# Softmax attention on one core: transposes in 32-bit words, a fused shift on GpSimd, and load groups of 8 heads

## The chip, the core and the metric

The kernel runs on one core of a Trainium2 chip. A core has five engines that run side by side, each with its own instruction queue: TensorE (PE; its weight loads are listed apart as PEld), VectorE (DVE), ScalarE (ACT), GpSimd (POOL) and SyncE (SP). In this kernel SP issues all transfers between the device's memory and the on-chip memory (SBUF). TensorE writes its results to PSUM, which VectorE and ScalarE can read; GpSimd works on SBUF alone. The metric is the time of one execution in microseconds on the device. Three runs of the kernel before gave 1264.91, 1265.55 and 1264.91 us, median 1264.91.

## The reference

```
B, H, Sq, Sk, D = 16, 32, 192, 1024, 128        # q, k, v are bf16
scale  = D ** -0.5
scores = einsum("bhqd,bhkd->bhqk", q, k) * scale
p      = softmax(scores, axis=-1)
out    = einsum("bhqk,bhkd->bhqd", p, v)
```

There are 16 x 32 = 512 heads. Each has 192 queries, 1024 keys and a depth of 128.

## The kernel before, in words

**Units.** Two heads a and b make a pair; there are 256 pairs, and each pair is three units of 128 query rows: the first 128 queries of a, the first 128 of b, and the last 64 of a together with the last 64 of b. That makes 768 units. In the third unit the two heads sit in the two column halves of TensorE (`tile_position`).

**What happens to a unit.** (1) `qk`: TensorE computes 128 x 1024 scores into one of two PSUM buffers `s_ps` (lines 215, 222, 228). (2) `rowmax`: VectorE multiplies them by minus the scale, writes them to SBUF as fp32 (`ss`), and keeps each row's minimum in `nb`, all in one instruction (line 300). (3) The shift: a unit of type W (the first two of a pair, `R_W`) has `nb` subtracted on GpSimd, which writes bf16 to `x_sb` (line 188); a unit of type E (the third, `R_EA`) gets its exponential on ScalarE, which also sums the rows into `rs` (line 356). (4) `tr`: TensorE transposes `x_sb` in eight 128 x 128 pieces of bf16 into one of two PSUM buffers `pt_ps`, by a matmul with the identity as the moving operand (line 244). Piece t holds every eighth key, from t on. (5) `evac`: ScalarE brings the transposed unit back to SBUF as `pt_sb`: type W with the exponential (line 367), type E as a copy (line 369). (6) `pv`: TensorE multiplies by V (lines 267, 273, 275), and for type W also by a column of ones, which gives the row sums (line 270). (7) `onorm`: once a pair is complete, VectorE takes two reciprocals of the row sums (line 327), waits for them, and multiplies the pair's 128 x 384 results by them into the output buffer `ob` (line 330).

**Order.** There is no planner; the order is written out by hand. TensorE goes through steps: in a step it issues the scores of the next unit, the transposes of the unit four steps back and the second matmul of the unit seven steps back. The lags `L_X, L_TR, L_EV, L_PV` are 2, 4, 5 and 7; the rings of buffers `ss`, `x_sb` and `pt_sb` have as many slots as the lags need. Semaphores tie the engines: scores of unit u wait for `rowmax` of u - 2, GpSimd waits for `rowmax` and for the transposes four units back, the second matmul of a pair's first unit waits for `onorm` two pairs back.

**Loads and stores.** SP works in groups of 16 heads (`G=16`), 32 groups, with two slots (`NS=2`). For each group it issues K as a transposing transfer of 4 MB (line 141), q as a transposing transfer (line 144), and V as a plain one of 4 MB (line 149), then the stores of an earlier group (lines 158, 163, 164). K and q of a group wait until the scores of the group two before have been computed, V until its second matmul has; the stores wait for `onorm`.

Of the kernel before, what the change touches and what calls it, by code (L numbers as in the profile page):

```python
# [6 lines left out]
F32 = mybir.dt.float32  # L7
ACT_FN = mybir.ActivationFunctionType
ALU = mybir.AluOpType

R_EA = 0
R_ED = 1
R_W = 2


def _attention_kernel(nc, q, k, v, out, G=16, NS=2, LAGS=(2, 4, 5, 7), ROUTES=(R_W, R_W, R_EA)):
# [4 lines left out]
    assert NH % G == 0 and G % 2 == 0  # L21
# [3 lines left out]
    NU = NGR * UPG  # L25
    KT_TILES = SK // 128
    scale = float(D) ** -0.5

    L_X, L_TR, L_EV, L_PV = LAGS
    assert 1 <= L_X < L_TR < L_EV < L_PV  # L30
# [4 lines left out]
    NRS = 4  # L35

# [5 lines left out]
    def route(u):  # L42
        return ROUTES[u % len(ROUTES)]

    x_cnt = []
    ev_cnt = []
    n_xa = n_xp = n_ea = n_ed = 0
    for u in range(NU):
        r = route(u)
        if r == R_W:  # L50
            n_xp += 1
            x_cnt.append(n_xp)
        else:
            n_xa += 1
            x_cnt.append(n_xa)
        if r == R_ED:
            n_ed += 1
            ev_cnt.append(n_ed)
        else:
            n_ea += 1  # L60
            ev_cnt.append(n_ea)

    with ExitStack() as es:
# [11 lines left out]
        vs = sb("vs", [128, NS, G, KT_TILES, 128], BF16)  # L75
        ob = sb("ob", [128, NSO, PPG, 4, 128], BF16)
# [3 lines left out]
        pt_sb = sb("pt_sb", [128, NPT, KT_TILES, 128], BF16)  # L80
# [3 lines left out]
        ident = sb("ident", [128, 128], BF16)  # L84
        s_ps = [ps("s_ps%d" % i, [128, SK], F32) for i in range(2)]
        pt_ps = [ps("pt_ps%d" % i, [128, KT_TILES, 128], BF16) for i in range(2)]
        o_ps = [ps("o_ps%d" % i, [128, 4, 128], F32) for i in range(2)]
        s_setup = sem("s_setup")
        sxk = [sem("sxk%d" % i) for i in range(NS)]
# [5 lines left out]
        s_xa = sem("s_xa")  # L95
        s_xp = sem("s_xp")
        s_tr = sem("s_tr")
        s_eva = sem("s_eva")
        s_evd = sem("s_evd")
# [6 lines left out]
        def unit_info(u):  # L106
            pr = u // 3
            k3 = u % 3
            g = pr // PPG
            pg = pr % PPG  # L110
            return pr, k3, g, pg

        O_SLOT = (0, 2, 1)

        def load_cnt(g):
            return 16 * (g // NS + 1)

        def store_cnt(g):
            return 48 * (g // NSO + 1)

        def wait_x(eng, u):
            if route(u) == R_W:
                eng.wait_ge(s_xp, x_cnt[u])
            else:
                eng.wait_ge(s_xa, x_cnt[u])

        def wait_evac(eng, u):
            if route(u) == R_ED:
                eng.wait_ge(s_evd, ev_cnt[u])
            else:  # L130
                eng.wait_ge(s_eva, ev_cnt[u])

        @block.sync
        def _(e):
            def loads(g):
                s = g % NS
                last_u = (g - NS + 1) * UPG - 1
                h0 = g * G
                if g >= NS:
                    e.wait_ge(s_qk, last_u + 1)  # L140
# [6 lines left out]
                if g >= NS:  # L147
                    e.wait_ge(s_pv, last_u + 1)
                e.dma_start(
                    vs[:, s], vf[h0:h0 + G].rearrange("g (p t) d -> p g t d", t=KT_TILES)  # L150
                ).then_inc(svl[s], 16)

            def stores(g):
                so = g % NSO
                e.wait_ge(s_on, (g + 1) * PPG)
                h0 = g * G
                og = of[h0:h0 + G]
# [10 lines left out]
            for g in range(NGR):  # L168
                if g + NS < NGR:
                    loads(g + NS)  # L170
                stores(g)
            for so in range(min(NSO, NGR)):
                n_uses = len(range(so, NGR, NSO))
                e.wait_ge(sst[so], 48 * n_uses)

        @block.gpsimd
        def _(gp):
            gp.memset(ones[:], 1.0).then_inc(s_setup, 1)
            gp.wait_ge(s_setup, 1)
            gp.affine_select(  # L180
                ident[:], ones[:], [[1, 128]], ALU.is_equal, 0.0, base=0, channel_multiplier=-1
            ).then_inc(s_setup, 1)

            def shift(u):
                gp.wait_ge(s_max, u + 1)
                if u >= NX:
                    gp.wait_ge(s_tr, u - NX + 1)
                gp.tensor_tensor(  # L188
                    x_sb[:, u % NX, :], ss[:, u % NSS, :],
                    nb[:, u % NSS: u % NSS + 1].to_broadcast([128, SK]), ALU.subtract,  # L190
                ).then_inc(s_xp, 1)

            for u in range(NU):
                if route(u) == R_W:
                    shift(u)

        @block.tensor
        def _(pe):
            def qk(u):
                pr, k3, g, pg = unit_info(u)  # L200
                s = g % NS
                if u % UPG == 0:
                    pe.wait_ge(sxk[s], load_cnt(g))
                    pe.wait_ge(sxq[s], load_cnt(g))
# [6 lines left out]
                for c in range(2):  # L211
                    cs = slice(512 * c, 512 * c + 512)
                    if k3 < 2:
                        x = a if k3 == 0 else b
                        ins = pe.matmul(  # L215
                            S[:, cs],
                            qt[:, s, x * SQ: x * SQ + 128],
                            kt[:, s, x * SK + 512 * c: x * SK + 512 * c + 512],
                            start=True, stop=True,
                        )  # L220
                    else:
                        pe.matmul(  # L222
                            S[0:64, cs],
                            qt[:, s, a * SQ + 128: a * SQ + 192],
                            kt[:, s, a * SK + 512 * c: a * SK + 512 * c + 512],
                            start=True, stop=True, tile_position=(0, 0),
                        )
                        ins = pe.matmul(  # L228
                            S[64:128, cs],
# [6 lines left out]
            def tr(u):  # L236
                wait_x(pe, u)
                if u >= 2:
                    wait_evac(pe, u - 2)
# [176 lines left out]
```

## Time and profile before

| what | value |
|---|---|
| median of the three runs | 1264.91 us |
| the profiled execution: span from first to last instruction | 1263.1 us |
| instructions recorded | 48,658, of them 40,960 on TensorE |
| mean granted TensorE clock | 0.999 |
| moved by transfers | 321.89 MB, mean 255 GB/s |

The profile is one execution taken apart. Busy time of an engine is the time in which at least one of its instructions is running. The chain of waits is followed back from the last instruction, at each step to what released it. A line such as "POOL x_sb L188 <- PE pt_ps L244: 266.8, 254, 1.1" says that line 188 on GpSimd stood idle 266.8 us in all, 254 times and at most 1.1 us, until line 244's matmul was done. A line of the timeline gives start, duration, engine, source line, operation and result<-inputs. In a table by stretches of time, each engine has its busy time and the number of its instructions, and then come the granted clock, the share of the transfer engines and the rate in GB/s.

### The profile page before, as it was taken

The numbers are of one execution on the slowest core, as the hardware profiler recorded it, in microseconds if no ns is written. First come the engines' busy times: TensorE is split into PE (matmuls) and PEld (weight loads), VectorE is DVE, ScalarE is ACT, GpSimd is POOL, SyncE is SP. The second block draws the span as 40 slices with busy tenths as digits, with TensorE's granted clock in tenths as the row PEclk, the third lists the DMA queues.
The fourth block names the chain that finished last, engine by engine and source line by source line (L and its number), as shares of the span: only waits on it lengthen the run. The fifth ranks groups of instructions, "written<-read, shape, count | busy, mean of one in ns | idle before, by whom it ended". The sixth has DMA issues, their size and how long they took to land.

```text
span 1263.1 us, 48658 instructions
## 1 busy us (share of the span) xinstructions
PE 1234.2 (98%) x20480; PEld 1009.4 (80%) x20480; DVE 1102.0 (87%) x2304; ACT 1048.6 (83%) x1281; POOL 960.4 (76%) x518
## 2 busy tenths in 40 slices
PE   3999999999999999999999999999999999999997
PEld 1888888888888888888888888888888888888886
DVE  2889888898988989898898988889898898989885
ACT  1888888888888888888888888888888888888886
POOL 2778777777877778787777877777787777878774
PEclk9999999999999999999999999999999999999999
DMA  9999999999999999999999999999999999999941
GB/s 288 268 261 240 278 280 266 288 270 245 254 269 261 279 233 255 281 275 262 261 230 272 271 276 268 252 251 272 272 267 281 253 263 252 271 261 281 244 118 27
DMA packets 790743, 321.89 MB, mean 255 GB/s; under 512 B 724992, under 2 KB 724992, under 8 KB 790528
## 3 DMA queue, kind: packets, MB, share of 16 engines
q1 hardware_dynamic: 790528, 318.78, 108.8%
q8 instruction: 164, 2.69, 0.8%
q14 instruction: 51, 0.42, 0.1%
HBM read 134.22 MB, written 25.17 MB: 126 GB/s over the span
## 4 chain that ended last, share of the span: by engine, by line
PE 97%; SPq 1%; DMA 1%; ACT 0%; issue 0%; DVE 0%; ACTq 0%
PE pt_ps L244 33%; PE o_ps L267 24%; PE s_ps L215 18%; PE o_ps L273 11%; PE s_ps L222 9%; SPq L141 1%; DMA vs<-in_v_dram 1%; PE o_ps L270 1%; PE o_ps L275 1%; SPq L144 0%; PE s_ps L228 0%; ACT x_sb L356 0%; ACT pt_sb L367 0%; DVE ob L330 0%; DVE rinv L327 0%
## 5 line engine op out<-in xcount | busy, mean ns | idle before, releaser
L188 POOL TENSOR_TENSOR x_sb<-ss,nb 128x1024 bf16<-128x1024 f32 x512 | 959.7, 1895 | 288.9 <-PE pt_ps L244 266.8
L300 DVE TENSOR_SCALAR_CACHE_REDUCE ss<-s_ps 128x1024 f32<-128x1024 f32 x768 | 938.5, 1222 | 140.5 <-PE s_ps L215 110.8
L244 PEld LDWEIGHTS pt_ps<-ident,x_sb 128*128 128x128 bf16 x6144 | 487.1, 148 | 203.3 <-issue 105.4
L367 ACT ACTIVATE pt_sb<-pt_ps 128x1024 bf16<-128x1024 bf16 x512 | 521.0, 1018 | 41.9 <-PE pt_ps L244 41.8
L244 PE MATMUL pt_ps<-ident,x_sb 128*128 128x128 bf16 x6144 | 520.7, 228 | 0.2 <-ACT pt_sb L367 0.2
L267 PE MATMUL o_ps<-vs,pt_sb 128*128 128x128 bf16 x4096 | 403.0, 217 | 0.3 <-DMA vs<-in_v_dram 0.3
L369 ACT ACTIVATE pt_sb<-pt_ps 128x1024 bf16<-128x1024 bf16 x256 | 262.1, 1024 | 140.1 <-PE pt_ps L244 140.0
L270 PE MATMUL o_ps<-ones,pt_sb 128*128 128x1 bf16 x4096 | 376.0, 165 | 0.0
L267 PEld LDWEIGHTS o_ps<-vs,pt_sb 128*128 128x128 bf16 x4096 | 352.3, 97 | 0.5 <-DMA vs<-in_v_dram 0.4
L270 PEld LDWEIGHTS o_ps<-ones,pt_sb 128*128 128x128 bf16 x4096 | 340.7, 96 | 0.0
L215 PE MATMUL s_ps<-kt,qt 128*128 128x512 bf16 x1024 | 305.3, 379 | 21.3 <-DMA qt<-in_q_dram 21.0
L356 ACT ACTIVATE x_sb<-ss,nb 128x1024 bf16<-128x1024 f32 x256 | 292.3, 1142 | 23.6 <-DVE ss L300 23.6
L273 PE MATMUL o_ps<-vs,pt_sb 128*64 128x128 bf16 x2048 | 162.3, 222 | 0.0
L275 PE MATMUL o_ps<-vs,pt_sb 128*64 128x128 bf16 x2048 | 162.3, 222 | 0.0
L222 PE MATMUL s_ps<-kt,qt 128*64 128x512 bf16 x512 | 153.2, 381 | 0.6 <-DVE ss L300 0.5
L228 PE MATMUL s_ps<-kt,qt 128*64 128x512 bf16 x512 | 153.2, 381 | 0.0
L330 DVE TENSOR_TENSOR ob<-o_ps,rinv 128x384 bf16<-128x384 f32 x256 | 142.7, 557 | 8.7
L273 PEld LDWEIGHTS o_ps<-vs,pt_sb 128*64 128x64 bf16 x2048 | 121.0, 109 | 17.1
L275 PEld LDWEIGHTS o_ps<-vs,pt_sb 128*64 128x64 bf16 x2048 | 121.0, 109 | 0.0
L215 PEld LDWEIGHTS s_ps<-kt,qt 128*128 128x128 bf16 x1024 | 63.3, 96 | 23.6 <-issue 21.5
L300 DVE DVE_READ_ACCUMULATOR ss<-s_ps 128x1 f32 x768 | 64.0, 83 | 0.0
L356 ACT ACTIVATION_READ_ACCUMULATOR x_sb<-ss,nb 128x1 f32 x256 | 48.9, 191 | 0.0
(11 smaller groups left out, 165.7 us busy)
## 6 DMA issues: line engine op xcount, KB each, us to landing
vs<-in_v_dram SPq DMA_DIRECT2D x32, 4096.0 KB, 15.2
out_dram<-ob SPq DMA_DIRECT2D x32, 512.0 KB, 15.9
out_dram<-ob SPq DMA_DIRECT2D x64, 128.0 KB, 4.9
kt<-in_k_dram SPq DMA_TRANSPOSE x32, 21.4
qt<-in_q_dram SPq DMA_TRANSPOSE x32, 6.6
```

Of the source, the lines that this page charges most:

```text
L188: gp.tensor_tensor(x_sb[:, u % NX, :], ss[:, u % NSS, :], nb[:, u % NSS: u % NSS + 1].to_broadcast([128, SK]), ALU.subtract,).then_inc(s_x ...
L215: ins = pe.matmul(S[:, cs], qt[:, s, x * SQ: x * SQ + 128], kt[:, s, x * SK + 512 * c: x * SK + 512 * c + 512], start=True, stop=True,)
L222: pe.matmul(S[0:64, cs], qt[:, s, a * SQ + 128: a * SQ + 192], kt[:, s, a * SK + 512 * c: a * SK + 512 * c + 512], start=True, stop=True, ...
L244: ins = pe.transpose(PT[:, t, :], X[:, t: SK: KT_TILES], ident[:])
L267: ins = pe.matmul(O[:, sl, :], PTS[:, t, :], vs[:, s, x, t, :], start=first, stop=last, skip_group_check=True)
L270: ins = pe.matmul(O[:, 3, sl: sl + 1], PTS[:, t, :], ones[:, 0:1], start=False, stop=last, skip_group_check=True)
L273: pe.matmul(O[0:64, sl, :], PTS[:, t, 0:64], vs[:, s, a, t, :], start=first, stop=last, skip_group_check=True, tile_position=(0, 0))
L275: ins = pe.matmul(O[64:128, sl, :], PTS[:, t, 64:128], vs[:, s, b, t, :], start=first, stop=last, skip_group_check=True, tile_position=(0, ...
L300: dve.tensor_scalar(ss[:, u % NSS, :], s_ps[u % 2][:], -scale, None, ALU.mult, ALU.min, accum_out=nb[:, u % NSS: u % NSS + 1],).then_inc(s ...
L356: act.activation(x_sb[:, u % NX, :], ss[:, u % NSS, :], ACT_FN.Exp, bias=nb[:, u % NSS: u % NSS + 1], scale=-1.0, accum_out=rs[:, pr % NRS ...
L367: act.activation(pt_sb[:, u % NPT], pt_ps[u % 2][:], ACT_FN.Exp, scale=-1.0).then_inc(s_eva, 1)
L369: act.activation(pt_sb[:, u % NPT], pt_ps[u % 2][:], ACT_FN.Copy).then_inc(s_eva, 1)
```

## The change

**32-bit transposes.** `x_sb` and `pt_ps` are looked at as 32-bit words of two bf16 values each, and a unit is transposed in four 128 x 128 pieces of fp32 with an fp32 identity. Piece t holds every fourth word, that is keys in pairs; a transposed row holds (even key, odd key) side by side for each query. The exponential of a type W unit separates them: it reads every second bf16 value and writes the even and the odd keys as blocks. A type E unit is copied as 512 int32 words, and its second matmul reads the weights with a stride of two instead.

**Self-test.** Before the first unit, GpSimd writes index patterns, TensorE transposes two blocks of them as fp32, ScalarE copies the result as words, and VectorE compares it with the pattern expected. The outcome, 1 or 0, is written into the matrix of ones that yields the row sums. TensorE's first scores wait for it.

**Shift.** GpSimd's subtraction becomes one instruction with one tensor input: times minus one, plus the row's `nb` taken as a per-partition operand. ScalarE's exponential of type W drops its scale of minus one.

**VectorE.** The reciprocals of a pair stay where they were in the order; the multiplication by them comes one step later, behind the next `rowmax`.

**Load groups.** K, q and V come in 64 groups of 8 heads with four slots (`G=8, NS=4`) instead of 32 groups of 16 with two. The stores stay at 16 heads (`GO=16`).

```diff
-def _attention_kernel(nc, q, k, v, out, G=16, NS=2, LAGS=(2, 4, 5, 7), ROUTES=(R_W, R_W, R_EA)):
+def _attention_kernel(nc, q, k, v, out, G=8, NS=4, GO=16, L_X=2, L_TR=4, L_EV=5, L_PV=7):
...
-        ident = sb("ident", [128, 128], BF16)
+        ident = sb("ident", [128, 128], F32)
...
-                stores(g)
+                if (g + 1) % (GO // G) == 0:
+                    stores((g + 1) // (GO // G) - 1)
...
+            gp.iota(za[:, 0], [[257, 128]], base=1, channel_multiplier=32767).then_inc(s_setup, 1)
+            gp.iota(zb[:, 0], [[32767, 128]], base=1, channel_multiplier=257).then_inc(s_setup, 1)
+            gp.iota(za[:, 1], [[257, 128]], base=1060000001, channel_multiplier=32767).then_inc(s_setup, 1)
+            gp.iota(zb[:, 1], [[32767, 128]], base=1060000001, channel_multiplier=257).then_inc(s_setup, 1)
...
-                gp.tensor_tensor(
+                gp.tensor_scalar(
                     x_sb[:, u % NX, :], ss[:, u % NSS, :],
-                    nb[:, u % NSS: u % NSS + 1].to_broadcast([128, SK]), ALU.subtract,
-                ).then_inc(s_xp, 1)
+                    -1.0, nb[:, u % NSS: u % NSS + 1], ALU.mult, ALU.add,
+                ).then_inc(s_x[W], 1)
...
-                X = x_sb[:, u % NX, :]
-                PT = pt_ps[u % 2]
-                ins = None
-                for t in range(KT_TILES):
-                    ins = pe.transpose(PT[:, t, :], X[:, t: SK: KT_TILES], ident[:])
+                ins = None
+                X = x_sb[:, u % NX, :].bitcast(F32)
+                PT = pt_ps[u % 2][:].bitcast(F32)
+                for t in range(T // 2):
+                    ins = pe.transpose(PT[:, 128 * t: 128 * t + 128], X[:, t::T // 2], ident[:])
...
+                if kind(u) == E:
+                    P = pt_sb[:, u % NPT].rearrange("p (t q y) -> p t y q", y=2, q=128)
+                else:
+                    P = pt_sb[:, u % NPT].rearrange("p (t y q) -> p t y q", y=2, q=128)
...
-            pe.wait_ge(s_setup, 2)
+            pe.wait_ge(s_setup, 6)
+            for i in range(2):
+                pe.transpose(
+                    pt_ps[0][:].bitcast(F32)[:, 128 * i:128 * i + 128], za[:, i].bitcast(F32), ident[:]
+                ).then_inc(s_probe, 1)
+            pe.wait_ge(s_probe, 7)
...
+            dve.tensor_tensor(
+                zd[:].rearrange("p a b -> p (a b)"), zc[:].rearrange("p a b -> p (a b)").bitcast(U16),
+                zb[:].rearrange("p a b -> p (a b)").bitcast(U16), ALU.not_equal,
+            ).then_inc(s_probe, 1)
...
+            dve.tensor_copy(ones[:], ze[:, 0:1].to_broadcast([128, 128])).then_inc(s_probe, 1)
...
                 u = step - L_PV - 1
                 if 0 <= u < NU and u % 3 == 2:
-                    onorm(u // 3)
+                    recip(u // 3)
+                u = step - L_PV - 2
+                if 0 <= u < NU and u % 3 == 2:
+                    norm(u // 3)
...
+            act.copy(zc[:].rearrange("p a b -> p (a b)"), pt_ps[0][:].bitcast(I32)[:, 0:256]).then_inc(s_probe, 1)
...
-                if route(u) == R_W:
-                    act.activation(pt_sb[:, u % NPT], pt_ps[u % 2][:], ACT_FN.Exp, scale=-1.0).then_inc(s_eva, 1)
+                if kind(u) == W:
+                    ins = act.activation(
+                        pt_sb[:, u % NPT].rearrange("p (t y q) -> p t y q", y=2, q=128),
+                        pt_ps[u % 2][:].rearrange("p (t q y) -> p t y q", y=2, q=128), ACT_FN.Exp)
                 else:
-                    act.activation(pt_sb[:, u % NPT], pt_ps[u % 2][:], ACT_FN.Copy).then_inc(s_eva, 1)
+                    ins = act.copy(pt_sb[:, u % NPT].bitcast(I32), pt_ps[u % 2][:].bitcast(I32))
+                ins.then_inc(s_ev, 1)
```

## The prediction

> **What bounds the kernel now.** I read the page first: busy times, then the chain that ended last.
>
> ```profile
> PE 1234.2 (98%) x20480; PEld 1009.4 (80%) x20480; DVE 1102.0 (87%) x2304; ACT 1048.6 (83%) x1281; POOL 960.4 (76%) x518
> ...
> PE 97%; SPq 1%; DMA 1%; ACT 0%; issue 0%; DVE 0%; ACTq 0%
> PE pt_ps L244 33%; PE o_ps L267 24%; PE s_ps L215 18%; PE o_ps L273 11%; PE s_ps L222 9%; SPq L141 1%; DMA vs<-in_v_dram 1%; PE o_ps L270 1%; PE o_ps L275 1%; SPq L144 0%; PE s_ps L228 0%; ACT x_sb L356 0%; ACT pt_sb L367 0%; DVE ob L330 0%; DVE rinv L327 0%
> ```
>
> TensorE carries the chain, a third of it in the transposes. In the chain in order of time the pattern repeats every 4.80 us per pair of heads (the same piece of transposes starts at 56.70, 66.30, 75.90: two pairs in 9.60), and 256 x 4.80 = 1229 of the 1263.1 us. The other engines wait for it:
>
> ```profile
> POOL x_sb L188 <- PE pt_ps L244: 266.8, 254, 1.1
> ACT pt_sb L369 <- PE pt_ps L244: 140.0, 253, 0.6
> DVE ss L300 <- PE s_ps L215: 110.8, 257, 22.1
> ```
>
> Per pair, POOL has 1.05 us to spare, ACT 0.70 (0.55 and 0.15) and VectorE 0.34.
>
> That is not the only bound. The timeline of SP's queue, which issues every load and store, shows one 16-head round (K, q, V, three stores, next K):
>
> ```profile
> 101.85 18.79 SPq L141 DMA_TRANSPOSE kt<-in_k_dram  x1
> 120.69 4.77 SPq L144 DMA_TRANSPOSE qt<-in_q_dram  x1
> 125.50 0.59 SPq L149 DMA_DIRECT2D vs<-in_v_dram  x1
> 126.14 4.29 SPq L158 DMA_DIRECT2D out_dram<-ob  x1
> 130.47 9.78 SPq L163 DMA_DIRECT2D out_dram<-ob  x1
> 140.29 0.63 SPq L164 DMA_DIRECT2D out_dram<-ob  x1
> 140.96 17.55 SPq L141 DMA_TRANSPOSE kt<-in_k_dram  x1
> ...
> 940.80 17.73 SPq L141 DMA_TRANSPOSE kt<-in_k_dram  x1
> ```
>
> No gap stands between them: each issue begins where the last ended, from 101.85 to 978. 22 rounds in 940.80 - 101.85 = 839 us are **38.1 us per round**; TensorE needs 8 x 4.80 = 38.4. Only after 978 does SP wait (2.6 and 2.4 us ahead of the K loads at 1055.14 and 1093.54, 5.9 us in all). So the transfers run 0.3 us per round behind being the bound themselves, and whatever TensorE gains beyond that meets them.
>
> What a round's transfers cost is read from short stretches (last column GB/s):
>
> ```profile
> 6.00:15.00 9.00, 0.00 (x0) 0.00 (x0) 0.00 (x0) 0.00 (x0) 0.00 (x0) 1.00 1.28 290
> 17.00:18.00 1.00, 0.00 (x0) 0.00 (x0) 0.00 (x0) 0.00 (x0) 0.00 (x0) 1.00 0.98 203
> 20.00:21.00 1.00, 0.00 (x0) 0.02 (x1) 0.00 (x0) 0.00 (x0) 0.00 (x0) 1.00 1.03 172
> 24.00:30.00 6.00, 5.59 (x24) 2.03 (x23) 5.36 (x11) 2.25 (x3) 5.87 (x4) 1.00 1.03 390
> 31.50:33.00 1.50, 1.43 (x16) 0.82 (x14) 1.50 (x3) 1.44 (x3) 1.10 (x1) 1.00 1.28 183
> ```
>
> K runs at 290, V at 390; at the borders K to q, q to V, V to K the rate falls to 203, 172 and 183. Inside a K load there are holes too (window 597 to 609 in 40 slices):
>
> ```profile
> GB/s 150 159 247 79 9 0 6 88 222 287 287 145 223 85 38 55 32 176 288 291 290 291 288 291 290 291 288 291 290 291 288 291 290 291 332 252 16 0 7 9
> ...
> q8 instruction: 164, 2.69, 0.8%
> ```
>
> The first K and q, issued while no engine computes, take 14.90 and 3.07 us; later medians are 17.9 and 4.0, 3.9 us more. The queue that fetches instructions moves 164 pieces of 16 KB, about one per 250 of TensorE's 40,960 instructions. 5.1 per round, 58% of them during K and q (22 of 38 us), make 1.3 us of hole for each. I take them as the holes' cause; that is an inference.
>
> **The change part by part.**
>
> *Transposes* (TensorE): 8 of 128 bf16 columns per unit become 4 of 128 fp32 columns. The present pitch: eight end in 0.66 us of which one takes 0.22, so 7 pitches in 0.43, 62 ns each, 0.50 us per unit. No fp32 matmul is in the trace. Lower end: the same 62 ns, since as many columns are loaded and as many rows stream. Upper end: four passes, that is the 512-row matmul L215, two in 0.43 us, 215 ns. In between, twice the bytes at the same byte rate gives 124. A pair then takes 4.80 - 3 x (0.496 - 4p): 4.06 at p = 62, 4.43 at 93, 4.80 at 124, 5.89 at 215. I take 93, between the nearest row and its byte-doubled form; anything up to 121 (4.77 per pair) is below the transfers.
>
> The stationary operand is the word-strided x. The trace speaks for some price there: the strided loads of L244 last 148 ns, the contiguous ones of L267 97. The Trainium skill's "TensorE: Matmul & The Clock Gate" (sections Weight-path perf modes and LDWEIGHTS) speaks against the change: fast weight load is not used for FP32, and a plain load costs columns / 1.2 ns. By it p would be about 107 (an estimate) and the pair 4.60; no run here shows it. The same page's Terms says that trn2's transpose mode is 4x faster for FP32, against the four passes.
>
> *Evacuations* (ACT). The exponential reads every second bf16. L356 reads twice the bytes per element, 1024 fp32, in 1142 ns with a pointer bias, L367 takes 1018; so I add nothing. Its ends are 1018 and twice that; twice would make ACT 4.10 + 2.04 = 6.1 us per pair. The copy handles 512 words instead of 1024: between 512 and 1024 ns, I take 600. ACT goes from 4.10 (1048.6 / 256) to 3.7 per pair, hidden by its 0.70 idle before and more now.
>
> *Second matmul.* Weights of the E unit are read with stride two; rows with stride eight still pitch at 62, E's pitch at 55: nothing, at most a few ns x 16.
>
> *GpSimd.* 1895 ns with two tensors becomes one tensor, two operations and a pointer. Ends: half (0.95) and, since nothing excludes a loss, twice (3.8). I take 1.9. Cover: 1.05 us per pair, gone at 2.4 us each (4.80 per pair).
>
> *VectorE.* The reciprocals move a step ahead of the multiply, so the 0.04 us wait between them disappears, and the multiply comes a step (about 1.5 us) later. Behind it waits the second matmul of the pair after next, two steps later: no wait. VectorE needs 4.80 - 0.34 = 4.46 per pair, minus 0.04; not the bound.
>
> *Self-test and start.* GpSimd's six setup operations (0.20 and 0.29 us shown, about 0.3 each: 1.8), two transposes, one ACT copy and four small VectorE operations (0.14 to 0.56 each) end near 5 us. They lie under the first load: K and q halve from 14.90 and 3.07, so the first scores can begin at about 12 instead of 21.0, and the first V is there at 18 instead of 33.2. The pipeline's seven steps of 1.5 fill until 22. TensorE's start is 11 us earlier. If the test lasted over 12 us, the excess would delay it, hidden still by the transfers.
>
> *8-head groups.* K, q and V are issued 64 times instead of 32; stores are unchanged, the buffers hold as many heads. Per round one more set of borders: K to q 1 x (1 - 203/290) = 0.3, q to V 0.5, V to K 0.6, sum 1.4 us (ends: 0 if the queue hides them, 1.6 with the V border at 390). I take 1.4 x 31 = +43 us. Against it, half of the 12,288 transpose instructions go: 25 fetches x 0.58 x 1.3 = -19 us (ends: 0 and -23, the latter if an fp32 transpose is fewer instructions still).
>
> **Sum.** Transfers bind, so I follow the last V. Before it lands at 1192.01 + 15.2 = 1207.2. SP's waits go: -5.9. Borders and fetches: +43 - 19. Lands at 1225. Then: its K and q were there 7 us earlier; 12 units instead of 24 remain, 11 x 1.45 = 16 to the last score, and 16.4 from there to the end (1246.7 to 1263.1 before): 25 us. Span 1250; the profiled execution's 1263.1 lies 1.8 below the median 1264.91, so **1252 us**. With the ends: 1205 (no border, -23) to 1278 (1.6 x 31, no fetch saved).
>
> **Rivals.**
> 1. *fp32 transposes are slow* (ends on the other side). TensorE stays the bound and the time is 1254 + 3.07 x (p - 124): from p = 128 it is slower than before; 1395 at 170, 1533 at four passes. For it: twice the bytes per element, strided loads already longer. Against: as many columns and rows per instruction.
> 2. *GpSimd becomes the bound.* From 2.45 us per operation; 1254 + 512 x (t - 2.4): 1561 at 3. For it: two operations in one. Against: one tensor read instead of two.
> 3. *The transfers yield.* If holes and borders both vanish, the round is 38.1 - 3.9 + 0 = 34.2 and VectorE's 4.42 x 256 = 1132 plus 12 before and 16 behind it binds: 1162; with half of it about 1190. For it: four slots let loads run further ahead. Against: SP is already ahead of need and never idle.
>
> **How the numbers follow.** Forecast 0.60 (its own range 1205 to 1278: 0.43 faster, 0.06 within, 0.11 slower), rival 1 0.27 (0.02, 0.01, 0.24), rival 2 with ACT's stride 0.07 (slower), rival 3 0.06 (faster). Faster 0.51, within 0.2% (about what a measurement can tell here) 0.07, slower 0.42. The range 1205 to 1395 leaves out rival 1 above p = 170 (0.13), most of rival 2 (0.04) and half of rival 3 (0.03).
>
> **What will show it.** Right: L141's rounds (two K loads) at 38.5 to 39.5 us with no gap, TensorE waiting for K or q at many group starts, transposes at a pitch below 121 ns, fetches near 140. Wrong: a pitch above 128 with POOL and VectorE waiting for pt_ps; POOL over 95% busy; rounds below 37.

## The result, and the profile after

The changed kernel takes 1296.7 us (median of four runs, 1291.3 to 1301.3). Against the kernel before the ratio is 1.0249, with a 95% interval from 1.0222 to 1.0275: it is slower by 2.5%. The profiled execution took 1291.3 us with a span of 1289.6; it is the shortest of the four, so the sums below explain 26.5 us of span (1289.6 against 1263.1) and a few microseconds less than the medians differ by.

The page of the kernel after: busy times, the chain that ended last by engine and by line, the queue that fetches instructions, and five groups (line, engine, operation, result<-inputs, shapes, count | busy us, mean ns of one | idle us before them and what ended most of it).

```profile
PE 1242.1 (96%) x17410; PEld 1018.0 (79%) x17410; DVE 1099.6 (85%) x2308; ACT 956.3 (74%) x1282; POOL 574.4 (45%) x522
...
q8 instruction: 140, 2.29, 0.7%
...
PE 79%; SPq 13%; DMA 5%; DVE 2%; issue 1%; DVEq 0%
...
L176 POOL TENSOR_SCALAR x_sb<-ss,nb 128x1024 bf16<-128x1024 f32 x512 | 572.9, 1119 | 700.7 <-PE pt_ps L226 613.8
L360 ACT ACTIVATE pt_sb<-pt_ps 128x1024 bf16<-128x1024 bf16 x512 | 523.7, 1023 | 173.6 <-PE pt_ps L226 173.5
...
L364 ACT COPY pt_sb<-pt_ps 128x512 int32<-128x512 int32 x256 | 150.0, 586 | 135.4 <-PE pt_ps L226 135.3
L321 DVE TENSOR_TENSOR ob<-o_ps,rinv 128x384 bf16<-128x384 f32 x256 | 141.6, 553 | 53.9 <-DMA out_dram<-ob 53.8
```

Three things are to be seen. GpSimd's and ScalarE's share of the work did become smaller (76% and 83% busy before), and both wait longer for TensorE's transposes. TensorE's busy time did not fall. And the chain, 97% of which lay on TensorE, now spends 18% in SP's queue and in stores. The last line of the fence says where that enters the core: the multiplication that writes `ob` waits 53.8 us for stores, which the kernel before never did.

One such wait, in the timeline of VectorE (start, duration, engine, line, operation, and in brackets the idle time before it and its releaser):

```profile
625.27 0.09 DVE L293 DVE_READ_ACCUMULATOR ss<-s_ps 128x1 f32 x1
629.58 0.56 DVE L321 TENSOR_TENSOR ob<-o_ps,rinv 128x384 bf16<-128x384 f32 x1 [4.22 <-DMA out_dram<-ob]
630.05 1.21 DVE L293 TENSOR_SCALAR_CACHE_REDUCE ss<-s_ps 128x1024 f32<-128x1024 f32 x1
```

SP's queue at the same moment:

```profile
597.61 16.77 SPq L125 DMA_TRANSPOSE kt<-in_k_dram  x1
614.42 1.47 SPq L128 DMA_TRANSPOSE qt<-in_q_dram  x1
615.93 0.58 SPq L133 DMA_DIRECT2D vs<-in_v_dram  x1
616.55 0.58 SPq L141 DMA_DIRECT2D out_dram<-ob  x1
617.18 8.81 SPq L146 DMA_DIRECT2D out_dram<-ob  x1
626.03 0.63 SPq L147 DMA_DIRECT2D out_dram<-ob  x1
626.71 8.14 SPq L125 DMA_TRANSPOSE kt<-in_k_dram  x1
```

The stores are issued behind K, q and V of two later load groups. The last of them has landed by 629.58; `ob` has two slots, so the first multiplication of an output group needs the stores of the group two before, and stands from 625.36 to 629.58. Behind it on VectorE stands the next `rowmax`, behind that the scores, and so TensorE. SP itself has no gap: it is issuing transfers all the time. Nor does it wait for an engine: in this trace the scores, second matmuls and multiplications that a load or a store waits for were done at least 27 us before it was issued, but for the last two groups of stores. The mean round of 16 heads (two K loads; rounds 3 to 25, counted from 0) is 39.5 us, where the kernel before took 38.1 (one K load).

The same can be followed at the end, in the chain in order of time (start, duration, what):

```profile
1245.59 0.71 SPq L141
1246.35 7.50 SPq L146
1253.89 3.10 DMA out_dram<-ob
1257.84 0.78 issue
```

The stores of output group 29, issued behind the last V, release its slot at 1257.0; the eight multiplications of group 31 run from 1257.01 to 1283.34, and the last store ends at 1289.6.

**Balance of the spans.** The first transposes start 8.3 us earlier (19.6 instead of 27.9; lines below), 256 undisturbed pairs of 4.787 us instead of 4.80 give 3.3, and 26.5 + 8.3 + 3.3 = 38 us of waits for transfers reach the end. They include what the granted clock adds: behind the four longest stands of TensorE after the start (2.6 to 3.6 us) it is at half for 3.4 to 6.8 us, 20.5 us in all.

The transposes themselves (one tile's instructions: ns minimum/median/maximum, first and last start in us); before and after:

```profile
L244 PEld LDWEIGHTS pt_ps<-ident,x_sb x6144: 141/147/171, 27.9 to 1253.8; 128*128 128x128 bf16 x199
L244 PE MATMUL pt_ps<-ident,x_sb x6144: 217/225/328, 27.9 to 1253.8; 128*128 128x128 bf16 x199
```

```profile
L226 PEld LDWEIGHTS pt_ps<-ident,x_sb x3072: 195/210/231, 19.6 to 1280.1; 128*128 128x128 f32 x192
L226 PE MATMUL pt_ps<-ident,x_sb x3072: 271/283/491, 19.6 to 1280.2; 128*128 128x128 f32 x192
```

Half as many, each longer. By the prediction's own formula, 4.787 = 4.80 - 3 x (0.496 - 4p) gives a pitch p of 123 ns; four in 0.64 us of which one takes 0.283 give 119. Twice the pitch of 62 is 124. So 32-bit transposes cost TensorE what the 16-bit ones did.

### The profile page after: what moved, and what is told of

It is laid out like the page before. It is cut to its first block, busy times and chain, and to the rows that moved or that the text cites. A ratio compares the mean times of both kernels' runs of the same rounds, so it can differ in the third digit from the quotient of the medians.

```text
span 1289.6 us, 42910 instructions
## 1 busy us (share of the span) xinstructions
PE 1242.1 (96%) x17410; PEld 1018.0 (79%) x17410; DVE 1099.6 (85%) x2308; ACT 956.3 (74%) x1282; POOL 574.4 (45%) x522
## 4 chain that ended last, share of the span: by engine, by line
PE 79%; SPq 13%; DMA 5%; DVE 2%; issue 1%; DVEq 0%
PE o_ps L249 29%; PE pt_ps L226 27%; PE s_ps L202 15%; SPq L146 10%; PE s_ps L210 8%; DMA out_dram<-ob 4%; DVE ss L293 2%; PE o_ps L255 1%; SPq L141 1%; SPq L125 1%; SPq L133 1%; SPq L128 0%; DMA qt<-in_q_dram 0%; DVE ob L321 0%; DVEq L112 0%
## 5 line engine op out<-in xcount | busy, mean ns | idle before, releaser
L176 POOL TENSOR_SCALAR x_sb<-ss,nb 128x1024 bf16<-128x1024 f32 x512 | 572.9, 1119 | 700.7 <-PE pt_ps L226 613.8
L360 ACT ACTIVATE pt_sb<-pt_ps 128x1024 bf16<-128x1024 bf16 x512 | 523.7, 1023 | 173.6 <-PE pt_ps L226 173.5
L226 PEld LDWEIGHTS pt_ps<-ident,x_sb 128*128 128x128 f32 x3072 | 469.3, 206 | 179.1 <-issue 107.7
L249 PE MATMUL o_ps<-vs,pt_sb 128*128 128x128 bf16 (+1 forms) x8192 | 569.6, 220 | 0.0
L226 PE MATMUL pt_ps<-ident,x_sb 128*128 128x128 f32 x3072 | 519.6, 292 | 0.0
L249 PEld LDWEIGHTS o_ps<-vs,pt_sb 128*128 128x128 bf16 (+1 forms) x8192 | 480.2, 104 | 30.9
L202 PE MATMUL s_ps<-kt,qt 128*128 128x512 bf16 x1024 | 306.8, 381 | 11.4 <-DMA qt<-in_q_dram 9.9
L364 ACT COPY pt_sb<-pt_ps 128x512 int32<-128x512 int32 x256 | 150.0, 586 | 135.4 <-PE pt_ps L226 135.3
L321 DVE TENSOR_TENSOR ob<-o_ps,rinv 128x384 bf16<-128x384 f32 x256 | 141.6, 553 | 53.9 <-DMA out_dram<-ob 53.8
L210 PE MATMUL s_ps<-kt,qt 128*64 128x512 bf16 x1024 | 155.8, 384 | 27.4 <-DVE ss L293 27.3
L202 PEld LDWEIGHTS s_ps<-kt,qt 128*128 128x128 bf16 x1024 | 62.7, 96 | 14.3 <-issue 12.2
L210 PEld LDWEIGHTS s_ps<-kt,qt 128*64 128x64 bf16 x1024 | 43.3, 110 | 32.0 <-DVE ss L293 31.8
L314 DVE RECIPROCAL rinv<-o_ps 128x2 f32<-128x2 f32 x256 | 42.5, 166 | 6.0 <-PE o_ps L249 6.0
## 6 DMA issues: line engine op xcount, KB each, us to landing
vs<-in_v_dram SPq DMA_DIRECT2D x64, 2048.0 KB, 10.1
out_dram<-ob SPq DMA_DIRECT2D x32, 512.0 KB, 10.6
```

The source lines that it names most:

```text
L176: gp.tensor_scalar(x_sb[:, u % NX, :], ss[:, u % NSS, :], -1.0, nb[:, u % NSS: u % NSS + 1], ALU.mult, ALU.add,).then_inc(s_x[W], 1)
L202: ins = pe.matmul(S[:, c:c + 512], qt[:, s, x * SQ: x * SQ + 128], kt[:, s, x * SK + c: x * SK + c + 512], start=True, stop=True,)
L210: ins = pe.matmul(S[r:r + 64, c:c + 512], qt[:, s, x * SQ + 128: x * SQ + 192], kt[:, s, x * SK + c: x * SK + c + 512], start=True, stop=T ...
L226: ins = pe.transpose(PT[:, 128 * t: 128 * t + 128], X[:, t::T // 2], ident[:])
L249: ins = pe.matmul(O[r:r + m, sl, :], P[:, t // 2, t % 2, r:r + m], vs[:, s, x, t, :], start=t == 0, stop=t == T - 1, skip_group_check=True ...
L321: dve.tensor_tensor(ob[:, so, pr % PPO, 0:3, :], o_ps[pr % 2][:, 0:3, 0:D], rinv[:, pr % 2, 0:3].unsqueeze(2).to_broadcast([128, 3, 128]), ...
```

## The experiments

The theory after the result: the transfers bind (one queue, no gaps), the load groups of 8 heads made their round longer, and the wait for `ob` is only the place where this reaches the engines. The rivals: **A**, something other than the grouping (the transposes, the moved multiplication) costs the time; **B**, two slots of `ob` are too few and the transfers as such would be quick enough.

**1. The change with its old load groups.**

```diff
-def _attention_kernel(nc, q, k, v, out, G=8, NS=4, GO=16, ...
+def _attention_kernel(nc, q, k, v, out, G=16, NS=2, GO=16, ...
```

> The changed kernel with load groups of 16 heads and two slots again, everything else of the change kept. Theory (the 8-head groups' extra borders lengthen the transfers' round from 38.1 to 39.5 us and the transfers bind): the round falls to about 37.6 us, below the 38.3 us that TensorE needs (8 pairs of 4.79), so TensorE binds again: 1260 us, within 3 us. Rival A (the 32-bit edits themselves lengthen the transfers): rounds stay above 39 us, 1280 us or more. Rival B (the store slots are the cause): 1275 us or more, since the stores stand at the same place.

Measured: 1261.27 us (eight runs, 1260.81 to 1261.75), ratio 0.9972 [0.9961, 0.9983]. A pair takes 4.787 us, no multiplication waits for stores, and from round 13 on SP has a gap again, 0.6 to 2.4 us ahead of 17 of the last 19 K loads:

```profile
619.59 10.02 SPq L146 DMA_DIRECT2D out_dram<-ob  x1
629.65 0.64 SPq L147 DMA_DIRECT2D out_dram<-ob  x1
631.05 17.51 SPq L125 DMA_TRANSPOSE kt<-in_k_dram  x1
```

From 630.29 to 631.05 SP waits for the scores of the group two before. Everything in the change except the grouping is worth 3.5 us together, which is the 3.3 of the pairs; the whole loss is the grouping's. A falls.

**2. The kernel before with the new load groups**, everything else as it was.

```diff
-def _attention_kernel(nc, q, k, v, out, G=16, NS=2, LAGS=...
+def _attention_kernel(nc, q, k, v, out, G=8, NS=4, GO=16, LAGS=...
+    PPO = GO // 2
+    NGO = NH // GO
...
-        ob = sb("ob", [128, NSO, PPG, 4, 128], BF16)
+        ob = sb("ob", [128, NSO, PPO, 4, 128], BF16)
...
-                stores(g)
+                if (g + 1) % (GO // G) == 0:
+                    stores((g + 1) // (GO // G) - 1)
```

> The kernel before with load groups of 8 heads and four slots (stores at 16 heads) and nothing else of the change. Theory: one more set of borders per round and no instruction fetches saved, so the round is 39.5 + 0.5 = 40 us and the time about 1305 us, slower than the changed kernel. Rival A (the 32-bit edits lengthen the transfers): rounds of 38.1 us, and a start 8 to 11 us earlier, 1252 to 1256 us. Rival B (store slots): as the changed kernel, near 1297 us, with VectorE waiting for the stores.

Measured: 1325.11 us (four runs, 1324.44 to 1329.85), ratio 1.0485 [1.0467, 1.0503]. The direction is the theory's, the size half as large again: 60 us. Its round is 40.4 us, 2.3 more than with groups of 16. In this kernel the reciprocal is the first to need the output's slot, and waits in the same way (engine, what waited <- for what: us in all, times, longest):

```profile
DVE rinv L329 <- DMA out_dram<-ob: 78.3, 27, 9.1
```

**3. Three slots of `ob`** in the changed kernel.

```diff
-    NSO = 2
+    NSO = 3
```

> The changed kernel with three slots for the output instead of two, so that the multiplication by the reciprocals need not wait for the stores of two groups back. Theory (the transfers bind): the waits for the stores vanish, but TensorE then waits for K and q of the next group instead; rounds stay at 39.5 us, the last V lands at 1255 us as now and 25 to 30 us of work follow it: 1280 to 1290 us. Rival B (the stores' place at the back of the queue is what costs): TensorE's 4.79 us per pair hold throughout and the start stays 8 us early: 1254 us.

Measured: 1299.78 us (four runs, 1292.45 to 1302.36), ratio 1.0267 [1.0236, 1.0299]. Neither expectation was met by its number, but B, which needed 1254, falls. The waits in the changed kernel and, below, with three slots:

```profile
POOL x_sb L176 <- PE pt_ps L226: 613.8, 489, 3.8
...
DVE ss L293 <- PE s_ps L202: 86.0, 223, 8.6
DVE ob L321 <- DMA out_dram<-ob: 53.8, 24, 5.0
```

```profile
DVE ss L293 <- PE s_ps L202: 138.8, 285, 8.5
PEld pt_ps L226 <- issue: 108.8, 271, 0.8
PEld s_ps L202 <- issue: 49.1, 29, 10.1
PE s_ps L202 <- issue: 35.8, 24, 3.4
```

The wait for the stores is gone. In its place TensorE stands ahead of the scores (L202) again and again; the longest, 10.1 us, is the start, the others come to 39 us in 28 waits on PEld and 35.8 on PE, which overlap. "issue" says only that the profile names no releaser, but the landings in the kept trace do: of the 22 waits of more than 0.6 us on PEld behind the start, 20 end 0.06 us after a group's q has landed. The round is 40.0 us. The wait has moved, the time has not; this is the picture that the prediction had expected for the changed kernel itself.

**4 and 5. The transfers alone**: the loads and stores of both groupings in their order, each load waiting only for the transfer that used its slot before; nothing is computed and zeros are stored.

```diff
-def _attention_kernel(nc, q, k, v, out, G=16, NS=2, GO=16, PAIRS=0):
+def _attention_kernel(nc, q, k, v, out, G=8, NS=4, GO=16, PAIRS=0):
```

> Transfers alone: all loads in groups of 16 heads and all stores in the order of the kernel before, no score, softmax or second matmul is computed and zeros are stored. Theory (instruction fetches make the holes in K and q, borders cost about 1.5 us per group): 38.1 less 3 x 1.3 for the fetches, a round of 34 us, about 1100 us in all. Rival (the transfers are as slow by themselves, holes come from elsewhere): 38 us per round, 1220 us.

> The same transfers alone in groups of 8 heads with four slots. Theory: the border set by itself, 1.5 to 2.0 us more per 16 heads than the groups of 16, so 45 to 65 us more in all. Rival (the borders cost nothing by themselves, only together with the computing): the same time within 10 us.

Measured in a single run each: 1075.24 us and 33.2 us per round with groups of 16; 1208.26 us and 37.3 per round with groups of 8. The same bytes, in the same queue, cost 133 us more, and with no engine at work; 45 to 65 had been expected. The rate shows where. Stretches of one round (from:to and length in us, GpSimd's busy time, granted clock, share of the transfer engines, GB/s), first with groups of 16, then with groups of 8:

```profile
303.00:314.00 11.00, 0.00 (x0) 1.00 1.28 290
315.00:317.00 2.00, 0.00 (x0) 1.00 1.04 201
318.00:320.50 2.50, 0.00 (x0) 1.00 0.93 256
...
323.00:330.00 7.00, 0.00 (x0) 1.00 1.01 385
330.00:331.00 1.00, 0.00 (x0) 1.00 1.17 307
```

```profile
309.00:310.00 1.00, 0.00 (x0) 1.00 0.86 186
310.50:314.00 3.50, 0.00 (x0) 1.00 0.80 207
317.50:319.50 2.00, 0.00 (x0) 1.00 1.26 128
320.00:326.00 6.00, 0.00 (x0) 1.00 1.27 290
```

In the middle of a load the rates are the same (290 for K). At the borders they fall: in the first to 201 where q begins and to 256 over 2.5 us from q into V; in the second to 186 where q begins, to 207 over 3.5 us from q into V, and to 128 for 2 us where the next K begins behind V. With groups of 16 the stores always stand between a V and the next K, and that stretch (330 to 331) runs at 307; with groups of 8 every other V is followed by a K at once.

**6. The same with instruction fetches**: the transfers of groups of 16 beside 20,480 matmuls on a constant tile, which wait for nothing and for which nothing waits.

```diff
-def _attention_kernel(nc, q, k, v, out, G=16, NS=2, GO=16, PAIRS=0):
+def _attention_kernel(nc, q, k, v, out, G=16, NS=2, GO=16, PAIRS=20480):
```

> The transfers alone in groups of 16 heads, beside a stream of 20,480 independent matmuls of 128 columns on one constant tile, which waits for no data (about as many TensorE instructions as the kernel before has, about 1270 us at 62 ns each). Theory (fetches of instructions make the holes): the round rises from about 34 to 38 us, and the holes are back. Rival (holes come from the semaphores, the compute engines' accesses or the transfers themselves): the round stays where it is without the stream.

Measured: 1216.78 us, 37.9 per round, with 160 pieces on the fetching queue:

```profile
q1 hardware_dynamic: 790528, 318.78, 113.0%
q8 instruction: 160, 2.62, 0.9%
```

160 pieces are 2.62 MB of 321, but they add 1215.0 - 1073.4 = 141.6 us of span: 0.89 us each. With them the round of the kernel before, 38.1, is reproduced without any of its data dependences. The packets of the kept traces show the same piece by piece. Averaged over the 126 pieces between 100 and 1000 us, the rate is 302 GB/s in the 2.5 us before a piece starts, 136 from 0.75 to 1.75 us behind its start, and 284 again from 2.5 us on; in the kernel before it is 292, 145 and 281. So the holes in the K loads, which the prediction put down to the fetches by inference, are theirs.

**7. Transposes of neighbouring words.** The only difference is the stride at which the stationary operand is read.

```diff
-                    ins = pe.transpose(PT[:, 128 * t: 128 * t + 128], X[:, t::T // 2], ident[:])
+                    ins = pe.transpose(PT[:, 128 * t: 128 * t + 128], X[:, 128 * t: 128 * t + 128], ident[:])
```

> The changed kernel, but each transpose takes 128 neighbouring words instead of every fourth, so that keys and rows of V no longer correspond (this part of the result is left wrong). If the stride of the weights sets the pitch of the 32-bit transposes (0.46 us of transposes per unit, some 115 ns each): the pitch falls towards 62 ns, the weight loads from 206 towards 140 ns. If the four-byte weight load or the pass of fp32 itself sets it: the pitch stays within 5 ns. The time, in both cases within 10 us of the changed kernel, since the transfers bind.

Measured in a single run: 1307.33 us. A pair takes 4.622 us where nothing disturbs it:

```profile
L226 PEld LDWEIGHTS pt_ps<-ident,x_sb x3072: 137/140/231, 19.4 to 1296.2; 128*128 128x128 f32 x192
L226 PE MATMUL pt_ps<-ident,x_sb x3072: 270/273/477, 19.4 to 1296.3; 128*128 128x128 f32 x192
```

and from the groups of its page:

```profile
L321 DVE TENSOR_TENSOR ob<-o_ps,rinv 128x384 bf16<-128x384 f32 x256 | 141.7, 553 | 96.1 <-DMA out_dram<-ob 96.0
```

The weight load falls from 210 to 140 ns and the pitch by the formula from 123 to 109. Of the two expectations on the pitch neither came: it falls by 14 ns, not towards 62 and not by less than 5. The gain of 256 x 0.165 = 42 us on TensorE doesn't reach the end: the wait for the stores grows from 53.8 to 96.0, by 42.2, and the round does not become shorter (40.0 us against 39.5). That shows most plainly that the transfers bind: a faster engine only waits longer. Why this one run is 10.6 us above the changed kernel's median isn't shown; within 10 had been expected.

The Trainium skill's "TensorE: Matmul & The Clock Gate", section LDWEIGHTS, gives a plain weight load as columns / 1.2 ns, which makes about 107 for 128 columns (an estimate). The pitch of 109 with neighbouring words agrees with it; the 123 with a stride of four, which the kernel uses, doesn't. The pair of 4.60 us estimated from that section is met only by the neighbouring words, with 4.622.

**8. V from a second queue.** In the changed kernel ScalarE's queue issues the loads of V, as soon as their slot is free; SP keeps K, q and the stores.

```diff
-                e.dma_start(
-                    vs[:, s], vf[h0:h0 + G].rearrange("g (p t) d -> p g t d", t=T)
-                ).then_inc(svl[s], 16)
...
+            def load_v(g):
+                if g >= NS:
+                    act.wait_ge(s_pv, (g - NS + 1) * UPG)
+                act.dma_start(
+                    vs[:, g % NS], vf[g * G:(g + 1) * G].rearrange("g (p t) d -> p g t d", t=T)
+                ).then_inc(svl[g % NS], 16)
...
+                if u % UPG == 2 and u // UPG + 1 < NS:
+                    load_v(u // UPG + 1)
+                if u >= NPT + 1 and (u - NPT) % UPG == 0 and (u - NPT) // UPG - 1 + NS < NGR:
+                    load_v((u - NPT) // UPG - 1 + NS)
```

> The changed kernel, still in load groups of 8, with the loads of V issued from ScalarE's queue instead of SP's. Theory (K, q, V and stores stand in one queue and the transfer engines run empty at each border between them): with a second queue the gaps are filled, the loads keep ahead, VectorE no longer waits for the stores, TensorE binds at 4.79 us per pair with its start 8 us early: 1252 to 1256 us. Rival (8-head pieces cost more by themselves, whatever the queue): rounds stay at 39 us or more, 1280 us or more.

Measured: 1278.03 us (median of seven runs: five from 1270.04 to 1279.35, two at 1292.14 and 1300.6), ratio 1.0067 [1.0038, 1.0096] by the five. That is between the two expectations. The waits for the stores are gone and pairs take 4.787 us, but the loads of V come at the wrong time. The first V runs beside the first K (376 GB/s from 7 to 8 us, V's rate, and 290 to 298 from 9 us on, K's); K's issue now lasts 14.21 us instead of 7.86, and the first scores begin at 19.64 us instead of 12.74; at pairs 13 and 29 TensorE stands for 6.0 and 10.1 us.

**9 to 11. Neighbouring words, with keys to match.** The transposes of experiment 7, and the scores' columns laid out so that keys and V rows correspond: TensorE reads K as its moving operand in pairs, each pair eight elements from the one before. With V from ScalarE's queue and groups of 8, the same with groups of 16, and groups of 16 with V from SP.

```diff
+                kp = [kt[:, s, x * SK:(x + 1) * SK].rearrange("d (p t y) -> d t p y", t=T // 2, y=2)
+                      for x in (a, b)]
...
+                    h = slice(c // 256, c // 256 + 2)
...
-                            kt[:, s, x * SK + c: x * SK + c + 512],
+                            kp[x - a][:, h],
```

> As v8, and the scores' columns are laid out so that each transpose takes 128 neighbouring words and the result stays right: the scores' matmul reads K as pairs of keys with a stride of eight. Theory: with the transfers out of the way the pair of 4.62 us seen with neighbouring words now counts: 1252 - 256 x 0.165 = 1210 us. Rival: reading K in pairs slows the scores' matmul (512 columns in more than 215 ns) and takes it back: 1252 us or more.

> As v8_perm in load groups of 16 heads. If the borders still cost with two queues, this beats v8_perm by 10 us or more; if they don't, it is 8 us slower, as its first scores come 8 us later: 1218 us.

> The changed kernel in load groups of 16 heads, one queue, with the scores' columns laid out for neighbouring words as in v8_perm. TensorE needs 8 x 4.62 = 37.0 us per round; the transfers took 37.3 us where they did not wait. Theory: the transfers bind again, 1225 to 1240 us. If the transfers have room that this trace doesn't show: 1219 us (1261 - 42).

Measured: 1576.51 (ratio 1.2451 [1.2433, 1.247]), 1589.91 (1.2558 [1.2539, 1.2576]) and 1578.34 (1.2466 [1.2447, 1.2485]). All three fail in the same way, seen in the scores' matmul of the kernel before and of the first of them:

```profile
L215 PE MATMUL s_ps<-kt,qt x1024: 376/377/634, 21.0 to 1245.2; 128*128 128x512 bf16 x171
L200 PE MATMUL s_ps<-kt,qt x1024: 608/630/636, 19.8 to 1557.1; 128*128 128x512 bf16 x171
```

A scores matmul with 512 columns takes 630 ns at the median instead of 377, and a pair 6.04 us. The saving at the transposes was bought with a stride at the moving operand that costs far more. What two queues or groups of 16 are worth these three can't tell, since TensorE binds in all of them.

**12. V from a second queue, but late.** As experiment 8, with each V issued six units ahead of its group's first unit on ScalarE, and the first once the first q has landed.

```diff
+            act.wait_ge(sxq[0], 16)
...
-                if u % UPG == 2 and u // UPG + 1 < NS:
-                    load_v(u // UPG + 1)
-                if u >= NPT + 1 and (u - NPT) % UPG == 0 and (u - NPT) // UPG - 1 + NS < NGR:
-                    load_v((u - NPT) // UPG - 1 + NS)
+                if u >= 0 and (u + 6) % UPG == 0 and (u + 6) // UPG < NGR:
+                    load_v((u + 6) // UPG)
```

> As v8 (groups of 8, V from ScalarE's queue), but each load of V is issued six units before the pair that needs it, and the first one only once the first q has landed, so that V does not run ahead of K. In v8 the steady pairs were 4.787 us and the loss stood in the first 200 us: first scores at 20.7 instead of 13.7 us and two stalls of 6 and 10 us. Theory: both go, 13.7 + 10.5 to the first second matmul, 256 x 4.787, and 6 us behind: 1256 us, faster than the kernel before and than groups of 16 (1261). Rival (two queues cost K more than the gaps they fill): stalls come back, 1265 us or more.

Measured: 1258.78 us (six runs, 1256.13 to 1263.03), ratio 0.9934 [0.9922, 0.9947], the best of all versions and faster than both kernels. The chain of the profiled run (1263.03 us) lies on TensorE again:

```profile
PE 94%; DMA 4%; SPq 1%; issue 0%; DVE 0%; ACT 0%
```

The first scores begin at 13.2 us, so that most of the early start of groups of 8 is kept; what is left of waits is 3.4 us near the start and 1.8 and 4.1 us later. So the cost of groups of 8 hardly reaches the end any more where V doesn't stand in one line with K, q and the stores. Whether the transfers themselves have become cheaper this doesn't show, since TensorE binds.

**13. Which part of the grouping costs?** The transfers alone in pieces of 8 heads, but in the order K, K, q, q, V, V, stores: as many pieces as in experiment 5, and as few changes of kind as in experiment 4.

```diff
-            def loads(g):
+            def load_k(g):
...
+            def loads(g):
+                for one in (load_k, load_q, load_v):
+                    one(g)
+                    one(g + 1)
```

> The transfers alone in pieces of 8 heads, but ordered K, K, q, q, V, V, stores, so that the borders between kinds are as few as with 16 heads. If the borders between kinds (q to V, and V to K without stores between) make the 133 us between the groups of 8 and of 16: close to groups of 16, 1073 to 1095 us. If the number and size of the pieces make it: close to groups of 8, 1190 us or more.

Measured: 1162.38 us, 36.1 per round: between the two expectations. This is one run, as are those it is compared with. Of the 4.1 us per round, the order of the kinds makes 1.2 (37.3 to 36.1), and the number or size of the pieces 2.9 (36.1 to 33.2). Here too the rate falls, but at q behind K, and through the start of V:

```profile
299.00:301.00 2.00, 0.00 (x0) 1.00 1.28 290
301.00:303.00 2.00, 0.00 (x0) 1.00 1.01 201
303.00:305.00 2.00, 0.00 (x0) 1.00 1.16 232
305.00:310.00 5.00, 0.00 (x0) 1.00 1.01 226
```

Why a border between two pieces of the same kind costs time stays open.

## Why the prediction was wrong

The forecast was 1252 us, faster; the kernel became slower. The mechanism that the prediction took as its base was right, and it is why its sum could be compared with the trace step by step: the transfers bind. Experiment 7 shows it directly.

**The step that failed is the border term** (0.3 + 0.5 + 0.6 = 1.4 us per round, with 1.6 as its upper end), and in it the border from q into V. Together with the fetches the term made 0.8 us per round; the rounds show 1.33 (38.16 to 39.49 in rounds 3 to 31). With the fetch term as measured (24 pieces fewer, 0.89 us each, 0.7 per round), the grouping costs 2.0 us per round in the changed kernel. It costs 2.3 in the kernel before and 4.1 in the transfers alone; why less beside the engines stays open.

The packets of the kept traces tell the borders apart. Take as lost what the time from one landing to the next has beyond the need of its bytes at 290 GB/s (K, q, stores) and 390 (V), averaged over 22 rounds. Experiment 2 differs from the kernel before in the grouping alone. Up to the landing of q it loses 0.2 us more per round (taken: 0.3), up to that of K 0.7 (taken: 0.6), up to that of V 1.6 (0.97 to 2.59; taken: 0.5), and the stores lose 0.2 less: 2.3 together. The changed kernel loses the same 2.59 up to V, and in the transfers alone V makes 2.7 of the 4.1 (0.68 to 3.40). So two of the three borders were taken about right, and the one from q into V costs three times what was taken.

The working had two faults. It read the borders in windows of 1 to 1.5 us at the kernel's start, between pieces of 16 heads, and counted a loss only there; with pieces of 8 the rate is low for longer, 207 GB/s over 3.5 us and 128 over 2 us in experiment 5. And it took it that the number of pieces matters only through the changes of kind, where experiment 13 finds some 70% of the loss in the pieces themselves. The chosen "ends" of 0 and 1.6 therefore didn't enclose the true value.

**The sum to the last V.** It was to land at 1225; issued at 1244.87, it did so 9.1 us later, at 1254. The 29 us are: 28 rounds from round 3's K load to round 31's, each 1.33 us longer instead of 0.8 (15); SP's 5.9 us of waits, which did go, but were a part of those rounds' pace before and no gain on top of it; a start that was 8 us behind by round 3's K load (109.79 instead of 101.85) where three rounds at 0.8 make 2 (6); and 2 more from the last round's K load to the landing of its V.

**The tail** was to be 25 us and took 36. The working let the last 12 units follow the last V's K and q. In fact TensorE was held by the stores: the last output group's eight multiplications could only begin at 1257.0, and needed 26.3 us and 6.2 to the end. The two misses, 29 and 11, are the 39.6 us between the forecast span of 1250 and 1289.6.

**Where the waits show** was wrong. TensorE was to wait for K or q at many group starts. The stores stand behind the loads of later groups in the same queue, and with two slots of `ob` they are needed sooner than those loads. Experiment 3 shows that this decided nothing about the time: take it away, and the waits at K and q appear as forecast, with the round at 40.0.

**The transposes**: taken at 93 ns, measured 119 to 123, at the upper of the two nearest values (124, twice the bytes at the same byte rate). "Anything up to 121 (4.77 per pair) is below the transfers" kept this from mattering to the forecast, and rightly: with 109 nothing is gained (experiment 7). But in a version where the transfers don't bind (experiment 1), it means that the main part of the change is worth 3 us and not the 95 of 256 x (4.80 - 4.43).

**What held.** Fetches: 140 pieces, 24 fewer, 21 us by experiment 6 against the 19 taken. The word copy: 586 ns against 600. The exponential that reads every second value: 1023 ns at the median before and after. The self-test: over at 5.2 us against about 5. GpSimd came out better than taken (1119 ns against 1900, with 950 as the lower end), and it is hidden as forecast. VectorE's moved multiplication added no wait of its own. Less exact: TensorE's start came 8.3 us earlier against 11, because only the issues halved: the first scores began 2.2 us after the end of q's issue before (18.83 to 21.01), and 2.6 after it now (10.19 to 12.74).

**The rivals.** Rival 1 (slow fp32 transposes) needed a pitch above 128 ns; it came within 5 to 9 of that, but it is not what happened: with those same transposes experiment 1 is faster than before. Rival 2 (GpSimd) falls at 45% busy. Rival 3 (the transfers yield) went the other way. Its price for a round without holes, 34.2, is close to the 33.2 of experiment 4, but nothing in the change takes all the fetches away.

What was missing is a rival in which the border costs more than 1.6 us. The point from which it decides could have been worked out: 1264.9 less 1252 is 12.9, or 0.42 per round, so that at 1.8 us nothing is gained. The 2.0 us measured give 1271, and SP's waits, the start and the tail named above make up nearly all of the rest.

## What to carry to other kernels

When one queue issues all transfers without a gap, as here, the engines' gains are worth nothing, and the granularity of the loads is a cost on the critical path. Look first for a gap ahead of the round's first load; if there is none, change the piece size alone before trusting a price for it: border losses read from a few short windows came out too small here (1.4 us per round against 2.0 and 2.3 in the two kernels), and the transfers run alone in both sizes gave too much (4.1), though they gave the direction. If smaller pieces are wanted for an early start, move one kind of load to another engine's queue, and issue it no earlier than it is needed.

## What the runs showed of the hardware

- A 32-bit transpose of 128 x 128 words has a pitch of 119 to 123 ns with words at a stride of four and about 109 with neighbouring words, against 62 for a bf16 one. Two of those are 124, so packing two bf16 values into a word halves the number of transposes and leaves their time within 4% (strided) or 12% (neighbouring). The stride costs 70 ns in the weight load (210 against 140) and 14 in the pitch.
- A matmul with 512 moving columns that are read in pairs with a stride of eight elements takes 630 ns at the median instead of 377. Strides cost at the moving operand too.
- In experiment 6 a piece of 16 KB on the instruction queue cost the transfers 0.89 us, some 14 times the 0.066 us that its bytes would need at 250 GB/s. 160 of them made 33.2 us of a round into 37.9, and the rate falls to less than half (302 to 136 GB/s) behind each.
- The same bytes in pieces of 8 heads instead of 16 took 12% longer in one queue with no engine at work (1208.26 against 1075.24 us). The largest part of it, 2.7 of 4.1 us per round, stands between the landings of q and V; why V begins so slowly behind a small q is open. That hardly any of the cost reaches the end when V comes from a second queue (experiment 12) is shown; that the second queue's transfers fill the holes of the first is only a likely reading.
- A plain V load on a second queue went ahead of the transposing K load that was issued at the same time: the first K's issue went from 7.86 to 14.21 us (experiment 8). Why the transposing transfer is the one to yield is open. The Trainium skill's "DMA: Bandwidth & Descriptors", section Queues, rings and completion order, says that a transfer engine takes turns between queues packet by packet, which, if nothing else decides, would favour the queue with the larger packets; no run here varied the size of the packets.
- GpSimd's subtraction with one tensor and a per-row operand takes 1119 ns where the form with two tensors took 1895, though it does two operations.
